# A table of due-time shifts per kind and stretch for a list-scheduled attention and two dense layers

## The chip, the cores and the metric

The kernel runs on one core of one Trainium2 chip. The metric is the device time of one execution in microseconds. Three executions of the kernel before took 1125.41, 1126.01 and 1126.11 us; their median is 1126.01 us.

## What is computed

Attention with normalised queries and keys, its output regrouped to 1792 tokens of width 768, and two dense layers of inner width 2048. All is float32, and the second dense layer takes the first one's output:

```python
attn = softmax(rmsnorm(q, g_q) @ rmsnorm(k, g_k).T / sqrt(64)) @ v   # 4 batches x 12 heads, 448 x 64
x = attn.transpose(0, 2, 1, 3).reshape(1792, 768)
h = x @ moe_w_in                   # 768 x 2048
x = (h * sigmoid(h)) @ moe_w_out   # 2048 x 768
h = x @ moe2_w_in
return (maximum(h, 0) ** 2) @ moe2_w_out
```

## The kernel before

**Numbers in two parts.** TensorE works on fp32r values, and a float32 operand is split into an upper part (a cast, line 578 on ScalarE or 580 on VectorE) and a lower part (operand minus upper part, line 587, on VectorE or GpSimd). A product is three matmuls: upper weight with upper data, lower weight with upper data, upper weight with lower data.

**Stages.** First the attention, 24 pairs of heads. Then the first dense layer in eight segments (two halves of the tokens by four quarters of the inner width), named `seg0` to `seg7` here. A segment has products into the inner width (lines 1082 and 1171), silu (1095, 1239), splits `g_hi`, `g_lo`, and products back (1269), whose sums go to a tile `part`. Then the second dense layer, two halves of the tokens, eight groups of 256 inner columns each: products (1171), relu (1437), square (1443, 1445), splits `h_hi`, `h_lo`, products back (1512, 1636), and `acc` (1528, 1531), which adds them to `gg`. Most products into the inner width come in sevens (`seven`, lines 1159 to 1219): seven half-sized products of sums of blocks stand for eight. `p1_copy` (566) takes the first one out of its bank, and `u_sum` (1186) adds the others from theirs; four tiles `g` hold the sums. The sums of the weights are `w_sum` (1128, 1147), and their parts are `w_hi`, `w_lo`. Sums of the data are `y_sum` (1322, 1376), and their parts are `y_hi`, `y_lo`. In the last group of all, 15 additions of kind `join` (1688) put partial sums together. The layers' raw weights are brought into shape by `magnitude` (980), `low` (985) and `merge` (992).

**Who sets the order.** Everything is first put down as steps of a `Plan` (lines 136 to 414). A step has a kind, a place `when` (a segment's number, or a nominal time in the second layer), the engines that may run it with a modelled duration on each, and the steps that it needs. `forward` (221) then issues them one by one. Of the steps whose needs are issued it takes the one with the earliest modelled start, and among equal starts the one with the smallest due time. That is line 262:

```python
k = (st, due[n], n)
```

So a due time decides only between steps that wait for a free engine together. Where a step may run on two engines, the other one is taken if it would end it earlier, and that comparison counts the steps ahead of it by due time. The loads `load_raw2` and `load_y` also don't start before their due time less 25 us (`hold`). `backward` (324) gives each step the time that it has left until the end, and `schedule` (372 to 405) goes through `forward` and `backward` eight times. Its due times are shifted by a table `DUE`, per kind and for four coarse stages, and the round with the shortest modelled span is kept. The attention's steps are pinned to nominal times and aren't ordered by due times. `issue` (407) emits the instructions in the order found, one fixed sequence for each engine; SyncE's queue carries nearly all DMAs in the same way.

**Buffers that matter below.** `p1` uses one PSUM bank of its own (bank 7, tag `pv`), the other products of a seven use three (`t`), products back use four (`s`). The split weights `w` have five buffers, the raw weights two.

Of the kernel before, what the change touches and what calls it, by code (L numbers as in the profile page):

```python
# [110 lines left out]
class Step:  # L111
# [18 lines left out]
    "now": {"ident": 5.75, "swap_pools": -0.5},  # L130
    "seg0": {"add": -0.5, "down": 3, "g_hi": 0.5, "g_lo": 0.75, "keep": 10.25, "load_raw": -6, "load_y": 0.5, "low": 1, "magnitude": -2, "merge": -6, "out1": -1, "p1_copy": 4, "part": 0.5, "prod": 4.75, "silu": 0.5, "store_y": -1, "u_sum": 2.75, "up": 2.5, "w_hi": 4.5, "w_lo": 6.25, "w_sum": -2, "y_hi": 0.75, "y_lo": 1, "y_sum": 2},
    "seg1": {"add": -4.25, "down": -4.5, "g_hi": 2.25, "g_lo": 5, "keep2": 45.25, "load_raw2": 6, "load_word": -5.5, "load_y": -0.75, "low2": -1.5, "magnitude2": -3, "merge2": -4.5, "p1_copy": -6.25, "part": -3.75, "prod": -3.25, "silu": -5.75, "store_y": 7, "u_sum": 2.25, "w_hi": 1.75, "w_lo": 1, "w_sum": -3, "y_hi": 10, "y_lo": 0.75, "y_sum": 2.5},
}


class Plan:
# [235 lines left out]
    def schedule(self):  # L372
        self.link()
        steps = self.steps

        at = [s.at for s in steps]
        due = [0.0] * len(steps)
# [17 lines left out]
        due = [d + x for d, x in zip(due, moved)]  # L395
        best = None
        got = [None]
        for _ in range(ROUNDS):
            got = self.forward(due, got[0])
            if best is None or got[0] < best[0]:  # L400
                best = got
            late = self.backward(got[1], got[2])
            due = [x - y for x, y in zip(moved, late)]
            self.log = getattr(self, "log", []) + [round(got[0], 1)]
        return best

    def issue(self):
        self.span, start, at, order = self.schedule()
# [1344 lines left out]
```

## Time and profile before

| | |
|---|---|
| median of three executions | 1126.01 us |
| the profiled execution's own time | 1125.93 us |
| its span, first to last instruction | 1124.2 us |
| TensorE busy | 1099.9 us, 98% |
| VectorE busy | 912.9 us, 81% |
| ScalarE busy | 617.2 us, 55% |
| GpSimd busy | 291.7 us, 26% |
| mean granted TensorE clock | 0.995 |

The profile comes from one execution. 1.73 us of that execution's time lie outside its span. A matmul's end is modelled and runs into the next one, so what counts for TensorE is the time in which nothing runs on it, and the distance from one start to the next. Attention takes up to 222.6 us of the span, the dense layers go from there to 1120.6 us, and what is left is the store of the last results. `seg1` lies at about 282 to 340 us, `seg2` at 340 to 396, `seg3` at 396 to 450, `seg4` from 450; the second layer begins at about 676 us, and its second half at about 900 us.

### The profile page before, as it was taken

What the parts mean: (1) busy time and instruction counts of PE and PEld (TensorE: products, weight loads), DVE (VectorE), ACT (ScalarE), POOL (GpSimd) and SP (SyncE); (2) the same over time, 40 slices, a digit from 0 to 9 for tenths busy, and PEclk for the clock granted to TensorE, in tenths of its full rate; (3) what the DMA queues carried; (4) which work ended last, traced back from release to release, by engine and by line L of the source; (5) the groups of instructions that cost most, each with busy time, mean ns of one, the idle gap of its engine ahead of it and who ended that gap; (6) DMA issues with size and microseconds to landing.
All of it is one profiled execution on the core that took longest, in us unless ns stands there. A gap on an engine that the chain in (4) does not pass through costs nothing.

```text
span 1124.2 us, 20358 instructions
## 1 busy us (share of the span) xinstructions
PE 1099.9 (98%) x7463; PEld 994.6 (88%) x7463; DVE 912.9 (81%) x1619; ACT 617.2 (55%) x1310; POOL 291.7 (26%) x369
## 2 busy tenths in 40 slices
PE   8999999999899999999999999999999999999998
PEld 6777777799798989999999998999999899999997
DVE  7999999767868689867777896688888967888886
ACT  7999999964534355455545534534333444333321
POOL 5789997300101113100000110010220201122220
PEclk9999999999999999999999999999999999999999
DMA  7344543397455658578777488778758784555544
GB/s 187 102 125 142 148 128 104 85 330 231 137 179 158 199 184 273 196 242 268 240 271 250 159 296 328 259 264 322 288 203 307 243 313 176 186 187 185 174 173 129
DMA packets 122435, 235.29 MB, mean 209 GB/s; under 512 B 12216, under 2 KB 86112, under 8 KB 122336
## 3 DMA queue, kind: packets, MB, share of 16 engines
q1 hardware_dynamic: 122096, 233.80, 62.4%
q8 instruction: 59, 0.97, 0.4%
q14 instruction: 40, 0.33, 0.1%
q10 hardware_dynamic: 240, 0.20, 0.1%
HBM read 157.58 MB, written 76.37 MB: 208 GB/s over the span
## 4 chain that ended last, share of the span: by engine, by line
PE 56%; DVE 6%; ACT 1%; issue 1%; DMA 0%; DVEq 0%; ACTq 0%
PE bank L1171 26%; PE bank L1269 13%; PE bank L1512 11%; PE bank L1636 7%; DVE w L587 1%; DVE g L1186 1%; DVE gg L1531 1%; DVE gg L1688 0%; ACT g L1437 0%; ACT g L1443 0%; DVE gl L587 0%; DVE W L1128 0%; DMA y<-g 0%; DVE W L1147 0%; DVE w L580 0%
## 5 line engine op out<-in xcount | busy, mean ns | idle before, releaser
L1269 PE MATMUL bank<-gg,w 128*128 128x448 f32 (+1 forms) x1168 | 238.3, 363 | 0.0
L1269 PEld LDWEIGHTS bank<-gg,w 128*128 128x128 f32 x1168 | 216.9, 188 | 16.8
L1186 DVE TENSOR_TENSOR g<-bank,g 128x448 f32<-128x448 f32 x180 | 109.1, 619 | 68.2 <-PE bank L1171 60.3
L1512 PE MATMUL bank<-w,gh 128*128 128x384 f32 (+1 forms) x564 | 143.7, 336 | 1.9 <-DVE gh L580 0.9
L1171 PE MATMUL bank<-yb,w 128*128 128x448 f32 (+1 forms) x548 | 121.1, 369 | 5.3 <-DVE w L587 2.4
L1171 PE MATMUL bank<-xb,w 128*128 128x448 f32 x528 | 116.2, 365 | 3.2 <-ACT g L566 3.2
L1531 DVE TENSOR_TENSOR gg<-bank,gg 128x384 f32<-128x384 f32 (+1 forms) x197 | 102.9, 548 | 20.0 <-PE bank L1512 19.7
L587 DVE TENSOR_TENSOR w<-W,w 128x768 fp32r<-128x768 f32 (+1 forms) x124 | 112.6, 915 | 5.3 <-ACT w L578 4.2
L1171 PEld LDWEIGHTS bank<-yb,w 128*128 128x128 f32 x548 | 102.8, 191 | 15.7 <-DVE w L587 4.0
L1171 PEld LDWEIGHTS bank<-xb,w 128*128 128x128 f32 x528 | 98.1, 188 | 11.7 <-ACT g L566 3.9
L1512 PEld LDWEIGHTS bank<-w,gh 128*128 128x128 f32 x564 | 102.4, 189 | 3.9 <-DVE gg L1531 1.6
L578 ACT CAST w<-W 128x768 fp32r<-128x768 f32 (+1 forms) x82 | 61.5, 750 | 77.9 <-PE bank L1269 21.1
L775 DVE TENSOR_REDUCE mx<-bank 128x1 f32<-128x448 f32 x168 | 96.5, 606 | 0.5 <-PE bank L753 0.5
L1512 PE MATMUL bank<-w,gl 128*128 128x384 f32 (+1 forms) x282 | 94.6, 335 | 1.9 <-DVE gl L587 1.9
L1437 ACT ACTIVATE g<-g 128x448 f32<-128x448 f32 x48 | 27.7, 578 | 123.7 <-DVE g L1186 123.3
L783 ACT ACTIVATE E<-bank,mx 128x448 f32<-128x448 f32 x144 | 93.4, 706 | 0.8 <-DVE mx L775 0.3
L1171 PE MATMUL bank<-xc,w 128*128 128x448 f32 x270 | 60.0, 366 | 0.0
L985 ACT ACTIVATE raw<-raw 128x768 int32<-128x768 uint16 (+1 forms) x72 | 59.2, 824 | 0.0
L587 POOL TENSOR_TENSOR gg<-g,gg 128x448 fp32r<-128x448 f32 x11 | 14.8, 1347 | 169.5 <-ACT gg L578 97.3
L753 PE MATMUL bank<-T 64*128 64x448 f32 x432 | 56.2, 390 | 2.1 <-ACT T L696 1.9
L587 POOL TENSOR_TENSOR gl<-g,gh 128x448 fp32r<-128x448 f32 (+1 forms) x18 | 18.9, 1052 | 150.9 <-ACT gh L578 82.3
L1512 PEld LDWEIGHTS bank<-w,gl 128*128 128x128 f32 x282 | 53.2, 188 | 2.6 <-DVE gl L587 2.6
(180 smaller groups left out, 2242.7 us busy)
## 6 DMA issues: line engine op xcount, KB each, us to landing
raw<-in_moe_w_in_dram SPq DMA_DIRECT2D x32, 768.0 KB
raw<-in_moe_w_out_dram SPq DMA_DIRECT2D x24, 512.0 KB
raw<-in_moe_w_out_dram SPq DMA_DIRECT2D x16, 768.0 KB
su<-w SPq DMA_DIRECT2D x16, 768.0 KB
w<-su SPq DMA_DIRECT2D x16, 768.0 KB
xf<-y SPq DMA_DIRECT2D x48, 224.0 KB
xf<-x SPq DMA_DIRECT2D x39, 224.0 KB
ki<-W SPq DMA_DIRECT2D x16, 384.0 KB
```

Source lines behind the costliest of these rows:

```text
L578: nc.scalar.copy(o(), a())
L587: kind, when, any_t(n, rate), lambda e: engine(e).tensor_tensor(o(), a(), h(), ALU.subtract),
L753: nc.tensor.matmul(pts[j].ap[:, :S], T.ap[r, 0, a, c * CQ:(c + 1) * CQ], T.ap[r, 1, b_], start=(k_ == 0), stop=(k_ == 2),)
L775: lambda e, pt=pt, mx=mx: nc.vector.tensor_reduce(mx.ap, pt.ap[:, :S], AX.X, ALU.max, negate=True),
L783: lambda e, j=j, n=n, pt=pt, mx=mx, E=E: nc.scalar.activation(E.ap[:, j], pt.ap[:, :S], AF.Exp, bias=mx.ap, accum_out=sums.ap[:, n:n + 1]),
L985: lambda e: nc.scalar.activation(lo(), raw.ap[:, :2 * m].bitcast(U16).rearrange("p (m t) -> p m t", t=4)[:, :, 1], AF.Copy, bias=2.0 ** -1 ...
L1171: nc.tensor.matmul(pt.ap[:, c1:c2], w_()[:, c0 + c, :], view(b, a, c)()[:, c1:c2], start=(start and c == 0 and k == 0), stop=(c == HC - 1 ...
L1186: lambda e: nc.vector.tensor_tensor(o.ap, pt.ap[:, :S], a.ap, ALU.add),
L1269: nc.tensor.matmul(pt.ap[:, c1:c2], w_()[:, f, :], gg.ap[:, k, a, f, c1:c2], start=(f == 0 and n == 0), stop=(f == HQ - 1 and n == 2), ski ...
L1512: nc.tensor.matmul(pt.ap[:, :en], g.ap[:, fi, c0:c0 + P], w_()[:, 0, e0:e0 + en], start=(n == 0), stop=(n == 5),)
L1531: "acc", at, dve_t(n), lambda e: nc.vector.tensor_tensor(o(), pt.ap[:, :n], o(), ALU.add),
L1636: nc.tensor.matmul(pt.ap[:, :NH], a[i][0](m), b[j][0](), start=(start and k == 0), stop=(k == 2), skip_group_check=True,)
```

## The change

A table `SHIFT` is added, with 363 entries in 27 stretches: the eight segments, and the second layer cut by nominal time into stretches of an eighth of one half, `end-2` to `end17`. After the eight rounds, `schedule` takes the due times with which the shortest round was made, adds each dense step's entry, runs `forward` once more, and returns that order, whatever its modelled span. A negative entry makes a step more urgent. The entries are between -406.5 and 328.25 us; 98 of them are at most 5 us in size and 140 are over 20. Attention's pinned steps have none. No step, operand, buffer or instruction is added or taken away. The core of the diff, with the stretches that are spoken of below:

```diff
+SHIFT = {
...
+    "seg1": {"add": -11.75, "down": -6, "g_hi": 148, "g_lo": -10.5, "keep": -27.75, "load_raw": -10.5, "low": -7.5, "magnitude": -17.25, "p1_copy": -4.25, "prod": 78.25, "u_sum": 123, "w_hi": 285.25, "w_lo": 29.75, "w_sum": -30.75},
+    "seg2": {"add": 1.5, "down": -99.75, "g_hi": 30, "g_lo": 8, "keep": 22.25, "load_raw": -18.75, "low": -73.75, "magnitude": -0.25, "merge": -0.25, "p1_copy": -42, "prod": 14.5, "silu": 17, "u_sum": 27.75, "w_hi": -10, "w_lo": -55, "w_sum": -52.75},
+    "seg3": {"down": -205.5, "g_hi": -6.5, "g_lo": 90.25, "keep": 33.25, "load_raw": 1.75, "low": -2.25, "magnitude": -1.25, "merge": -26.5, "out1": -8.5, "p1_copy": -9.5, "prod": 86, "silu": -1.75, "store_y": 4.5, "u_sum": -384.5, "w_hi": -37.75, "w_lo": 31.75, "w_sum": 1.75},
+    "seg4": {"down": 9.25, "g_hi": -0.75, "g_lo": -3.25, "keep2": -23.75, "load_raw2": -7.25, "load_word": -15, "load_y": 8, "low2": 2.25, "magnitude2": 1, "merge2": 10.5, "p1_copy": 28.25, "part": 13.5, "prod": 2, "silu": -2, "w_hi": -2.75, "w_lo": 10.75, "w_sum": -13.5, "y_hi": 15.5, "y_lo": -406.5, "y_sum": 155},
+    "seg5": {"add": -41, "down": 69.5, "g_hi": 72.25, "g_lo": 2.5, "keep2": -16, "load_raw2": -136.75, "load_word": -5.5, "low2": 77.25, "magnitude2": -29.5, "merge2": 163.25, "p1_copy": 3.5, "prod": 29, "silu": 10, "u_sum": -10.5, "w_hi": 17.75, "w_lo": 10.25, "w_sum": -101.75},
...
+    "end0": {"acc": 0.5, "down2": 3, "h_lo": -10.25, "load_word2": 4.25, "load_y": 4.5, "p1_copy": 4.25, "prod": 57, "relu": 13, "square": 6.75, "u_sum": 0.75, "w_hi2": -3.25, "w_lo2": 3.5, "w_sum": 14.75, "y_hi": 19.75, "y_lo": 21.5, "y_sum": -3.75},
...
+    "end7": {"acc": 53.25, "down2": 5, "h_lo": -12.25, "keep_parts2": -9.5, "load_word2": -11.75, "p1_copy": 0.75, "relu": -7, "square": 75, "u_sum": 29.25, "w_hi2": -5.75, "w_lo2": -18.75, "w_sum": 5.25},
+    "end8": {"down2": -9, "h_hi": 3, "h_lo": -3.25, "load_word2": 47, "load_y": 5, "relu": -7.5, "square": 1, "store": -13.5, "w_hi2": -36.5, "y_hi": 45.75, "y_lo": 53.75, "y_sum": 0.25},
...
+    "end16": {"acc": -38.5, "down2": -62.25, "h_hi": -1, "h_lo": -4.25, "join": 1.5, "load_parts2": 0.5, "p1_copy": 3, "prod": -30.5, "relu": -1.75, "u_sum": 20},
...
 }
...
         for _ in range(ROUNDS):
-            got = self.forward(due, got[0])
+            end = got[0]
+            got = self.forward(due, end)
             if best is None or got[0] < best[0]:
-                best = got
+                best, args = got, (due, end)
             late = self.backward(got[1], got[2])
             due = [x - y for x, y in zip(moved, late)]
             self.log = getattr(self, "log", []) + [round(got[0], 1)]
-        return best
+        def part(s):
+            when = s.when[0]
+            if s.nom is not None or when not in ("seg", "end"):
+                return None
+            return when + str(int(s.when[1] if when == "seg" else s.when[1] * 8 / self.turn))
+
+        due, end = args
+        return self.forward([d + SHIFT.get(part(s), {}).get(s.kind, 0.0) for s, d in zip(steps, due)], end)
```

## Rows read from the trace of the kernel before

**Rows 1.** The page's head: each engine's busy time, its share of the span, instructions.

```profile
PE 1099.9 (98%) x7463; PEld 994.6 (88%) x7463; DVE 912.9 (81%) x1619; ACT 617.2 (55%) x1310; POOL 291.7 (26%) x369
```

**Rows 2.** Busy time by stretch; each starts A:B length, then PE, PEld and the rest.

```profile
222.60:1120.60 898.00, 883.54 (x4557) 825.71 (x4557) 710.25 (x1225) 402.68 (x685) 126.31 (x99) 1.00 0.68 230
508.00:676.00 168.00, 168.00 (x847) 156.02 (x846) 135.61 (x225) 84.81 (x133) 14.50 (x10) 1.00 0.75 246
957.00:1091.00 134.00, 134.00 (x709) 125.62 (x709) 110.83 (x215) 45.71 (x85) 28.36 (x28) 1.00 0.53 183
```

**Rows 3.** Waits of PE in the dense layers (total, times, longest us), largest first.

```profile
PE bank L1171 <- ACT g L566: 3.2, 2, 2.5
PE bank L1171 <- DVE w L587: 2.8, 3, 1.9
PE bank L1171 <- ACT g L1437: 2.1, 1, 2.1
PE bank L1512 <- DVE gl L587: 1.9, 1, 1.9
```

**Rows 4.** Busy time around two falls of the clock; PEclk is third from last.

```profile
302.80:306.20 3.40, 3.40 (x11) 3.04 (x10) 2.28 (x4) 2.60 (x5) 0.00 (x0) 0.50 0.23 45
306.20:309.60 3.40, 3.40 (x19) 3.11 (x19) 2.62 (x5) 0.00 (x0) 1.15 (x1) 1.00 0.60 197
691.90:695.30 3.40, 3.40 (x12) 3.13 (x11) 3.40 (x8) 2.31 (x4) 0.00 (x0) 0.50 0.21 87
```

**Rows 5.** Timeline at the longest wait, in seg1: start, length, engine, instruction, [idle before].

```profile
301.33 2.51 PE L1171 MATMUL bank<-xb,w 128*128 128x448 f32 x9 [2.51 <-ACT g L566]
...
300.01 0.83 ACT L578 CAST w<-W 128x768 fp32r<-128x768 f32 x1
300.75 0.53 ACT L566 COPY g<-bank 128x448 f32<-128x448 f32 x1
```

**Rows 6.** Timeline at the wait in seg2, ScalarE.

```profile
357.31 0.82 ACT L578 CAST w<-W 128x768 fp32r<-128x768 f32 x1
358.11 0.53 ACT L566 COPY g<-bank 128x448 f32<-128x448 f32 x1
```

**Rows 7.** Timeline at the wait in seg3, VectorE.

```profile
413.34 0.62 DVE L587 TENSOR_TENSOR gg<-g,gg 128x448 fp32r<-128x448 f32 x1
413.88 0.55 DVE L1147 TENSOR_TENSOR W<-W 128x384 f32<-128x384 f32 x1
414.35 0.62 DVE L1186 TENSOR_TENSOR g<-bank,g 128x448 f32<-128x448 f32 x1
```

**Rows 8.** Timeline at the wait where seg4 begins: PE's wait, and VectorE ahead of it.

```profile
450.62 0.48 PE L1171 MATMUL bank<-gh,w 128*128 128x224 f32 x2 [0.37 <-DVE w L587]
...
449.08 0.62 DVE L1376 TENSOR_TENSOR xf<-xf 128x448 f32<-128x448 f32 x1
449.61 0.95 DVE L587 TENSOR_TENSOR w<-W,w 128x768 fp32r<-128x768 f32 x1
```

**Rows 9.** Timeline at the wait before the second layer's second half, VectorE.

```profile
887.21 1.14 DVE L1186 TENSOR_TENSOR g<-bank,g 128x448 f32<-128x448 f32 x2
888.28 0.54 DVE L1531 TENSOR_TENSOR gg<-bank,gg 128x384 f32<-128x384 f32 x1
888.74 0.60 DVE L1186 TENSOR_TENSOR g<-bank,g 128x448 f32<-128x448 f32 x1
889.27 0.60 DVE L587 TENSOR_TENSOR gl<-g,gh 128x448 fp32r<-128x448 f32 x1
```

**Rows 10.** Timeline at 753 us: VectorE beside GpSimd, and PE's wait behind them.

```profile
752.62 1.40 POOL L587 TENSOR_TENSOR v<-W,v 128x384 fp32r<-128x384 f32 x1
...
753.06 1.77 DVE L587 TENSOR_TENSOR w<-W,w 128x768 fp32r<-128x768 f32 x1
...
755.35 0.62 PE L1512 MATMUL bank<-w,gh 128*128 128x384 f32 x2 [0.48 <-DVE gg L1531]
```

**Rows 11.** Waits in SyncE's queue in the dense layers (total, times, longest us).

```profile
SPq L973 <- DVE W L992: 123.5, 31, 8.8
```

19 lines of the change are left out of this document (added).

## The prediction

> **What bounds the kernel now.** First the page's head: TensorE is busy for 98% of the span, VectorE for 81%, ScalarE for 55% [rows 1]. That share alone does not say how much is left, because a matmul's modelled end runs into the next one. So the second view is busy time by stretch. In the dense part, 222.6 to 1120.6 us, TensorE runs 4557 matmuls and is busy for 883.54 of 898.00 us [rows 2]. The 14.46 us that are missing are all that an order of the same matmuls can win from waits. They are not spread evenly: from 508 to 676 us and from 957 to 1091 us, 302 us together, nothing is missing at all [rows 2]. There a new order can only keep the time or lose some.
>
> The third view is the waits of PE. Ten groups hold the dense part's waits, and the four in rows 3 carry most of them. Four single waits are long: 2.5, 2.1, 1.9 and 1.9 us, 8.4 us of the 14.46 [rows 3]. In each TensorE stands for one late step on ScalarE or VectorE, not for a DMA. The fourth view is the granted clock. It is at full speed but for two stretches of some 3.4 us, at 302.8 and 691.9 us, where it is 0.50, the lower level of 1.2 GHz. In these 11 and 12 matmuls start, against 19 in the same time behind the first of them [rows 4]. Eight matmuls at 3.40 / 19 = 0.18 us each make about 1.4 us lost in each, 2.8 in both. The first fall begins 1.5 us after the end of the longest wait, at 301.33 us [rows 5], and the second stands behind the wait of 2.1 us at the second layer's start; behind the two of 1.9 us there is none. So the dense part has 14.46 + 2.8 = 17.3 us to win, 1.5% of the span, and attention has nothing in this change, since its steps are pinned.
>
> **The change, part by part.** It adds and removes no instruction, so the 4557 matmuls cost what they cost. The front end of the sum is therefore fixed, and only waits and clock can move. What moves is who goes first when several steps wait for one engine. I can't see the new order, but at each wait I can read which step was late, what stood just ahead of it on its engine, and whether the two entries of the table turn that pair round. The time of what stood ahead, from start to start, is then what the late step gains at most.
>
> At 301.33 us, in `seg1`, PE waits 2.51 us for a copy of a bank, `p1_copy` [rows 5]. Just ahead of it ScalarE runs an upper part of weights, `w_hi`, from 300.01 to 300.75, so 0.74 us. The table has -4.25 for the one and +285.25 for the other: the pair turns. Gain 0.74, and the wait falls to 1.8. That is the length after which the clock stayed up elsewhere, so I count the first fall of the clock as gone, 1.4 more. In `seg2` it is the same pair: 357.31 to 358.11 us is 0.80 [rows 6], the entries are -42 and -10, and PE's wait there is what is left of the group of 3.2 us beside the 2.5: 0.7 [rows 3]. Gain 0.7. In `seg3` PE waits 1.9 us for a lower part of weights, `w_lo` [rows 3]. Ahead of it VectorE has a `g_lo` (0.54 us from start to start), a `w_sum` and a `u_sum` [rows 7]. Only the `g_lo` falls behind (+90.25 against +31.75), while `u_sum` with -384.5 stays ahead for certain. Gain 0.54. Where `seg4` begins, `w_lo` (+10.75) stands behind a `y_sum` (+155) of 0.53 us, and PE's wait is 0.37 [rows 8]. Gain 0.37. Before the second layer's second half PE waits 1.9 us for an `h_lo` [rows 3]. Its group starts at 7 times 27.6 us of nominal time, which is `end7`, while its relu, square and splits lie in `end8`. VectorE runs three `u_sum` (887.21 to 888.28 and 888.74 to 889.27, 1.60 us) and an `acc` ahead of it [rows 9]. The entries are +29.25 for `u_sum` and -3.25 for `h_lo`: it passes all three. Gain 1.60, if its upper part is ready by then.
>
> Two waits are not helped. At the second layer's start PE waits 2.1 us for a relu [rows 3], and `end0` makes relu later by 13 us while squares get 6.75 and splits 0 or less: nothing gained there, and the second fall of the clock stays. In the last group `u_sum` gets +20 against +1.5 for `join`, which holds the final chain's sums behind the additions; I price it at nothing, because the chain has the last matmuls in front of it, and at up to 1 us if that cover is gone.
>
> The queues behind the moved steps: each engine runs its own fixed sequence, so a step that is put ahead and isn't ready yet holds all behind it. SyncE's loads move too: in `seg5` the raw loads may be issued 136.75 us sooner. They still wait for one of two raw buffers, as they do now, 31 times and 8.8 us at the longest [rows 11], and the y loads and stores stand behind them. I cost that at nothing, because the waits of PE have no DMA in them now; the bound is one wait of 8.8 us less whatever lead those loads have.
>
> One row bears on GpSimd. At 753.06 us VectorE's `w_lo` takes 1.77 us while GpSimd works beside it, against 0.95 for the same shape alone [rows 8, 10], and PE then waits 0.48 us for the `acc` behind it [rows 10]. The Trainium skill, page "SBUF — State Buffer", section "Who interferes with whom", says that a VectorE instruction with two SBUF inputs and a GpSimd one that reads SBUF share one read port, and that whichever starts first keeps it for its whole length. By that rule a table that moves splits and sums between the two engines can slow VectorE without adding an instruction; it makes the third rival below.
>
> The sum, against the profiled execution's own 1125.93 us, which stands 0.08 us under the median: 0.74 + 1.4 + 0.7 + 0.54 + 0.37 + 1.60 = 5.35 us. 1125.93 - 5.35 = 1120.6 us.
>
> **The rivals.** *Nearly all waits go.* The table has an entry for almost every kind, and the order is rebuilt from the front, so waits that I gave nothing for can go as well. Three quarters of the 17.3 us are 13.0: 1112.9 us. For it: most of the waits are shorter than two VectorE instructions. Against it: the second layer's start, which the table doesn't help.
>
> *Nothing that can be measured.* Due times decide only among steps with one modelled start. If the late steps weren't yet waiting in the plan when the ones ahead were chosen, the pairs above don't turn, and waits go in one place and come in another: about 1125.5 us. For it: PE's waits are where the chip departs from the plan, since a plan would not choose to wait 2.5 us in one place.
>
> *GpSimd takes more steps.* If ten more collisions like that at 753 us stand uncovered, each costs PE 0.48 us: 4.8 us, which eats the gain: about 1125.4 us. For it: GpSimd is busy 126 of the 898 us, so there is room [rows 2]. Against: its waits of PE number one now.
>
> *Slower: heads of queues in the full stretches.* The mechanism is a step that the table has put ahead on VectorE or ScalarE, whose input comes late on the chip and which holds steps behind it that TensorE needs. The place is the 302 us in which no time is missing now [rows 2]; the entries there are large (`seg5` has `g_hi` at +72, `low2` at +77, `merge2` at +163). The price is that of the four long waits, 2.1 us each, and 1.4 for a fall of the clock behind each second one. The Trainium skill, page "TensorE: Matmul & The Clock Gate", section "Architectural detail: the array is 16× 32×32, not 1× 128×128", says that ScalarE and VectorE take their instructions strictly in order, which speaks for this rival; no row here shows an instruction overtaken. It decides from four such waits on: 8.4 + 2.8 = 11.2 less the 5.35 is +5.9 us, 1131.8 us. With two, 4.2 + 1.4 = 5.6 just cancels the gain. Against it: VectorE has 32 of 168 and 23 of 134 us free there [rows 2], so a held step mostly finds slack.
>
> That the change doesn't act is hardly possible: `forward` runs once more with the shifted due times and its order is returned even if the modelled span is longer.
>
> **How the numbers follow.** The forecast of 1120.6 us has a chance of 0.48, nearly all waits going 0.11, nothing measurable 0.13, GpSimd 0.06, slower 0.22. A measurement of this kernel can tell about 0.2%, 2.3 us, from no change. So faster is 0.48 + 0.11 = 0.59, the same 0.13 + 0.06 = 0.19, slower 0.22. The forecast's own range runs from 1116 (twice the gain, less a little) to 1123.5. The range for 8 in 10 goes from 1112, where three quarters of what can be won are won, to 1130, just over where three of the four waits of the slower rival come (6.3 + 2.1 - 5.35 = 3.1 us more); it leaves out the deepest gains and the heavier half of the slower case.
>
> **What would show it.** Right: TensorE's idle time in the dense part falls from 14.46 to about 10.5 us; one fall of the clock is left, at the second layer's start; the waits for `p1_copy` in `seg1` and `seg2`, and that before the second half, are shorter or gone; the two full stretches stay full. Wrong: new waits of PE in these stretches, a third fall of the clock, more and longer VectorE instructions beside GpSimd, or a wait of PE behind a DMA. If idle time falls where the pairs didn't turn, the forecast may be right in size and its steps wrong.

## The result, and the profile after

Four executions of the changed kernel took 1114.12 to 1116.25 us, median 1114.99; four of the kernel before, beside them, 1125.89 in the median. The ratio is 0.9905, 95% interval 0.9887 to 0.9922: 10.9 us faster. The forecast was 1120.6, so the direction held, the time lies in the range, and the gain was twice what was forecast. The profiled execution of after took 1114.12 us, its span is 1112.3, and its mean granted clock 0.998; the other three had 0.997, 0.995 and 0.995. One execution of a later kernel, raw_moved, took 1534 us at a mean clock of 0.654 and is left out of its median.

First the page's head of after, against [rows 1]: the same 7463 matmuls, and each engine's busy time within 2%.

```profile
PE 1094.0 (98%) x7463; PEld 991.0 (89%) x7463; DVE 910.7 (82%) x1629; ACT 615.9 (55%) x1308; POOL 287.0 (26%) x361
```

Then the stretches of after, as [rows 2] are those of before (A:B, length, PE, PEld, DVE, ACT, POOL, granted clock, DMA share, GB/s).

```profile
222.60:1108.70 886.10, 878.72 (x4572) 823.91 (x4569) 706.15 (x1231) 402.37 (x684) 121.50 (x91) 1.00 0.68 232
508.00:676.00 168.00, 166.99 (x840) 154.43 (x839) 133.77 (x220) 80.34 (x127) 25.74 (x18) 1.00 0.75 248
957.00:1091.00 134.00, 133.31 (x714) 126.64 (x713) 113.92 (x219) 45.55 (x87) 37.09 (x34) 1.00 0.52 179
```

In the dense part TensorE now lacks 7.38 us, where it lacked 14.46, and no fall of the clock lies in it in this execution, where there were two [rows 4]. The second and third line are the stretches in which nothing was missing before: 1.01 and 0.69 us are missing now.

The five largest groups of waits of PE in the dense layers of after (total, times, longest). Line numbers of after are those of before plus 38: 1209 stands for 1171, 1550 for 1512.

```profile
PE bank L1209 <- DMA w<-sw: 2.0, 1, 2.0
PE bank L1307 <- DVE gg L625: 1.4, 2, 1.0
PE bank L1674 <- DVE part L625: 1.2, 3, 0.7
PE bank L1550 <- DVE gh L618: 0.9, 1, 0.9
PE bank L1209 <- ACT g L1277: 0.5, 1, 0.5
```

None of the four groups of [rows 3] is left; the longest wait is a new one, for a DMA. What a wait costs is best read from the starts of the matmuls on both sides of it, less the usual distance of two starts (203 ns for 448 columns, 174 for 384). By that measure, place by place:

| place (us where the wait begins in before) | before | after |
|---|---|---|
| start of the dense layers, 222.7 | 0.8 | 0, but it starts 1.1 later |
| seg1, 286 | 1.5 | 0 |
| seg1, 298 | 2.7, and a fall of the clock | 0.6 |
| seg2, 358 | 0.8 | 0 |
| seg3, 414 | 2.1 | 1.8 in three waits, at 424 to 428 |
| seg4, 450 | 0.5 | 0 |
| seg7, 648 in after (full before) | 0 | 1.2 |
| second layer's start, 689 | 2.3, and a fall of the clock | 0 |
| 729, 754, 832 | 1.6 in three | 0 |
| ahead of the second half, 888 | 2.0 for an `h_lo` | 2.1 for a load, at 876 |
| second half | 2.8 in four | 3.9 in seven |

The waits sum to 17.1 us before and 9.6 after, the two falls to 2.8 and 0. That is 10.3 us of the 13.0 by which the dense part is shorter; most of the rest lies in starts that are 0.02 to 0.25 us late: 57 in before, which sum to 5.3 us, and 40 in after, which sum to 3.5. 1.1 us are lost again because attention ends later.

Why it ends later shows in its last stretch. Before and after, TensorE waits there for a reciprocal, `sum`, on VectorE; the first line is of before, the others are of after, the last of them a stretch as above:

```profile
218.50 0.22 PE L823 MATMUL bank<-ident,sum 64*7 64x64 f32 x2 [0.40 <-DVE sum L830]
...
215.02 1.39 DVE L618 CAST w<-W 128x768 fp32r<-128x768 f32 x1
216.45 0.96 DVE L625 TENSOR_TENSOR w<-W,w 128x768 fp32r<-128x768 f32 x1
...
218.77 0.22 PE L861 MATMUL bank<-ident,sum 64*7 64x64 f32 x2 [1.74 <-DVE sum L868]
...
219.20:222.60 3.40, 3.40 (x20) 2.01 (x18) 1.48 (x5) 1.95 (x3) 0.00 (x0) 0.51 0.53 192
```

The splits of a dense weight now stand on VectorE ahead of attention's last steps, and the clock is 0.51 behind the wait. All nine kernels in which entries of `seg0` for the engines' steps are in force wait 1.73 to 1.85 us there, the eleven others 0.40 or 0.41. `rest`, which has this wait and no fall of the clock up to there, starts its first dense product at 222.23 us; turned, which has neither, at 221.23. So these entries cost 1.0 us ahead of the dense layers, and a fall of the clock where one comes.

### The profile page after: what moved, and what is told of

The parts are those of the page before. It is cut to its first block, busy times and chain, and to the rows that moved or that the text cites. A ratio compares the mean times of both kernels' runs of the same rounds, so it can differ in the third digit from the quotient of the medians.

```text
span 1112.3 us, 20308 instructions
## 1 busy us (share of the span) xinstructions
PE 1094.0 (98%) x7463; PEld 991.0 (89%) x7463; DVE 910.7 (82%) x1629; ACT 615.9 (55%) x1308; POOL 287.0 (26%) x361
## 4 chain that ended last, share of the span: by engine, by line
PE 87%; DVE 7%; issue 2%; ACT 1%; DMA 1%; SPq 0%; POOL 0%; DVEq 0%; ACTq 0%
PE bank L1209 29%; PE bank L1307 20%; PE bank L1550 13%; PE bank L901 7%; PE bank L1674 6%; PE bank L791 4%; PE bank L834 3%; PE bank L1120 3%; PE bank L725 2%; DVE g L1224 1%; PE bank L798 1%; DVE w L625 1%; DVE gg L625 1%; DVE W L1030 1%; DMA w<-sz 0%
## 5 line engine op out<-in xcount | busy, mean ns | idle before, releaser
L1209 PE MATMUL bank<-yb,w 128*128 128x448 f32 (+1 forms) x548 | 118.1, 363 | 0.5 <-ACT g L1277 0.5
L616 ACT CAST w<-W 128x768 fp32r<-128x768 f32 (+1 forms) x86 | 64.4, 752 | 96.2 <-PE bank L1550 28.1
L625 DVE TENSOR_TENSOR w<-W,w 128x768 fp32r<-128x768 f32 (+1 forms) x121 | 105.8, 880 | 6.0 <-ACT w L616 4.9
L625 POOL TENSOR_TENSOR gl<-g,gh 128x448 fp32r<-128x448 f32 (+1 forms) x16 | 14.6, 914 | 188.3 <-ACT gh L616 110.1
L625 POOL TENSOR_TENSOR gg<-g,gg 128x448 fp32r<-128x448 f32 x6 | 7.9, 1315 | 183.7 <-ACT gg L616 176.3
L1209 PEld LDWEIGHTS bank<-xc,w 128*128 128x128 f32 x270 | 50.7, 188 | 4.3
```

The source lines that it names most:

```text
L616: nc.scalar.copy(o(), a())
L625: kind, when, any_t(n, rate), lambda e: engine(e).tensor_tensor(o(), a(), h(), ALU.subtract),
L1209: nc.tensor.matmul(pt.ap[:, c1:c2], w_()[:, c0 + c, :], view(b, a, c)()[:, c1:c2], start=(start and c == 0 and k == 0), stop=(c == HC - 1 ...
```

## The experiments

Each kernel is compared with runs of the kernel before on the same chip; both medians stand in the table, and a gain or loss in us is their difference. "Idle" is TensorE's idle time from 222.60 us to 3.60 us ahead of the span's end, in the one profiled execution: 14.46 in before, 7.38 in after. In turned, only_dma and group the dense layers begin 1.1 to 1.5 us sooner, so their first wait, 0.5 us, lies ahead of that stretch.

| kernel | time, us | before, us | ratio to before, 95% | idle |
|---|---|---|---|---|
| seg_only | 1121.88 | 1125.66 | 0.9966 [0.9954, 0.9978] | 10.25 |
| end_only | 1125.39 | 1125.66 | 1.0002 [0.9993, 1.0012] | 16.12 |
| pairs | 1138.28 | 1125.66 | 1.0121 [1.0106, 1.0136] | 22.95 |
| rest | 1125.05 | 1125.66 | 1.0003 [0.9993, 1.0012] | 13.63 |
| w_hi_later | 1126.87 | 1125.93 | 1.0008 [0.9996, 1.0019] | 15.04 |
| seg_and_y | 1120.41 | 1125.93 | 0.9958 [0.9943, 0.9973] | 9.52 |
| no_y | 1122.06 | 1125.93 | 0.9969 [0.9959, 0.9980] | 11.65 |
| shuffled | 1174.38 | 1125.93 | 1.0432 [1.0411, 1.0453] | 46.79 |
| raw_behind | 1122.13 | 1125.30 | 0.9973 [0.9963, 0.9983] | 12.72 |
| to_end8 | 1117.12 | 1125.30 | 0.9923 [0.9910, 0.9937] | 8.34 |
| no_dma | 1134.71 | 1125.30 | 1.0078 [1.0064, 1.0092] | 20.12 |
| only_dma | 1123.72 | 1125.30 | 0.9984 [0.9975, 0.9993] | 12.01 |
| turned | 1122.14 | 1126.12 | 0.9965 [0.9952, 0.9978] | 12.98 |
| relu_up | 1125.30 | 1126.12 | 0.9994 [0.9983, 1.0005] | 14.05 |
| raw_moved | 1126.10 | 1126.12 | 0.9998 [0.9986, 1.0011] | 14.39 |
| turned_relu | 1122.87 | 1126.12 | 0.9975 [0.9965, 0.9986] | 13.69 |
| group | 1121.35 | 1125.84 | 0.9961 [0.9947, 0.9974] | 11.71 |
| after_g_lo | 1114.79 | 1125.84 | 0.9901 [0.9888, 0.9915] | 7.46 |

### Halves of the table, and the forecast's ten entries

**seg_only** keeps the entries of the first layer, **end_only** those of the second.

```diff
 # seg_only; end_only is the other way round
-    "end-2": {"load_y": -17.25, "y_hi": 328.25, ...},
+    "end-2": {},
...
```

> Only the eight segments' entries; the second layer has none. In the traces of before and after, starts of matmuls come 10.9 us too late in all between 222 and 676 us before, and 4.8 us after. If the stretches act each by itself, this run keeps the 6.1 us of the first layer and nothing else: about 1119.8 us, with the wait of 2.1 us and the fall of the clock at the second layer's start still there. If the entries of both layers only work together (the second layer's steps are fitted to an order that this kernel also has at their start), the second layer may wait more than before: 1122 us or over.

> Only the second layer's entries. From 676 us on, matmuls start 14.4 us too late in all before and 8.1 us after. If the stretches act each by itself: 6.3 us faster than before, about 1119.6 us, with the waits of 2.5, 0.7, 1.9 and 0.4 us in seg1 to seg4 as before and no fall of the clock at the second layer's start. If the entries need each other: less than half of that, 1123 us or over.

Neither half is worth what was expected, and together they are worth three times the sum of what they are alone: 3.8 and 0 us. Up to seg7 seg_only has nearly the waits of after (one of 0.45 us, at 594, is its own); then the wait at seg7's end, 1.0 us in after and none in before, is 3.7. Its largest group of waits of PE:

```profile
PE bank L1307 <- DVE gg L625: 4.0, 2, 3.7
```

end_only has the waits of before up to 450 us, each the same within 0.02 us from start to start. The wait at the second layer's start is gone from it, but 2.0 us come at 744, 1.1 at 782, 1.7 at 804 and 2.2 for a load at 888.

**pairs** has only the ten entries whose pairs the forecast counted, **rest** all but these.

```diff
 # pairs: all that is left of the table
+    "seg1": {"p1_copy": -4.25, "w_hi": 285.25},
+    "seg2": {"p1_copy": -42, "w_hi": -10},
+    "seg3": {"g_lo": 90.25, "w_lo": 31.75},
+    "seg4": {"w_lo": 10.75, "y_sum": 155},
+    "end7": {"u_sum": 29.25},
+    "end8": {"h_lo": -3.25},
```

> Only the ten entries on which the forecast's sum rests: p1_copy and w_hi of seg1 and seg2, g_lo and w_lo of seg3, y_sum and w_lo of seg4, u_sum of end7, h_lo of end8. If a wait shortens because the step just ahead of the late one falls behind it: 5.35 us faster than before, about 1120.5 us, and those five waits shorter by 0.74, 0.7, 0.54, 0.37 and 1.6 us. If the two steps of a pair weren't waiting together when the planner chose, the pairs don't turn: the five waits stand at their places as before, or others come with a changed order, and the time is 1125 us or over.

> The whole table without those ten entries. If the forecast's pairs carry 5.35 of the 10.9 us: about 1120.3 us, with the five waits back. If what works is the order that all entries make together: at most a few of the five waits are back, the wait at the second layer's start stays away, and the time is 1115 to 1118 us.

The ten entries that the forecast credited with 3.95 us and a fall of the clock made the kernel 12.6 us slower, and the other 353 alone gain nothing. In the timeline of pairs at the longest wait, in seg1 (start, length, engine, instruction, idle before), against [rows 5]:

```profile
301.38 1.15 DVE L625 TENSOR_TENSOR gg<-g,gg 128x448 fp32r<-128x448 f32 x2
301.43 0.55 ACT L616 CAST gg<-g 128x448 fp32r<-128x448 f32 x1
301.88 0.83 ACT L616 CAST w<-W 128x768 fp32r<-128x768 f32 x1
302.45 0.61 DVE L606 COPY g<-bank 128x448 f32<-128x448 f32 x1
303.12 1.86 PE L1209 MATMUL bank<-xb,w 128*128 128x448 f32 x4 [3.63 <-DVE g L606]
```

`w_hi` did go later. But a `g_hi` took its place on ScalarE, and `p1_copy` went to VectorE instead, behind two `g_lo`: the wait for it grew from 2.51 to 3.63 us. An entry of the table doesn't simply turn a pair. It changes what the planner takes next among all the steps that wait, and on which engine.

### The pairs turned by hand

**turned** therefore turns the same five pairs in the finished order of before. No table; every other instruction keeps its place on its engine.

```diff
+TURN = [
+    (1947, "ahead", 1944),   # seg1: p1_copy ahead of w_hi
+    (2121, "ahead", 2118),   # seg2: p1_copy ahead of w_hi
+    (2265, "behind", 2293),  # seg3: g_lo behind w_lo
+    (2468, "behind", 2495),  # seg4: y_sum behind w_lo
+    (3901, "behind", 3900),  # end7: h_lo ahead of the three u_sum
+    (3903, "behind", 3901),  # end7: u_sum behind h_lo
+]
```

> The kernel before's order with nothing but the forecast's five pairs turned by hand: in seg1 and seg2 p1_copy ahead of w_hi on ScalarE, in seg3 g_lo behind w_lo on VectorE, where seg4 begins y_sum behind w_lo, before the second layer's second half h_lo ahead of the three u_sum. No table, and no other step moves. If the forecast's terms were sized rightly and only the way from an entry of the table to a turned pair was wrong: PE's waits there fall from 2.5, 0.7, 1.9, 0.4 and 1.9 us by 0.7, 0.7, 0.5, 0.4 and 1.6, the fall of the clock behind the first goes in most executions, and the time is the forecast's 1120.6 us (1119.5 to 1122). If a turned pair only hands the wait to the step that is now behind, as in the kernel that had these entries alone: 1125 us or more, with new waits of PE just behind the five places.

It is 4.0 us faster, between the two that were expected. The terms can be read one by one (start to start). seg1: 2.68 to 1.86, but 0.47 come right behind it. seg2: 0.83 stays. seg3: 2.07 to 1.39. seg4: 0.53 to 0.41. Ahead of the second half: 2.04 to 0.95, but 0.29 and 1.57 come behind. The timeline of turned in seg1, in seg2, and twice ahead of the second half:

```profile
298.53 0.51 ACT L566 COPY g<-bank 128x448 f32<-128x448 f32 x1
298.94 0.84 ACT L578 CAST w<-W 128x768 fp32r<-128x768 f32 x1
299.09 2.09 PE L1171 MATMUL bank<-xb,w 128*128 128x448 f32 x9 [1.70 <-ACT g L566]
...
301.69 1.48 PE L1171 MATMUL bank<-yb,w 128*128 128x448 f32 x6 [0.31 <-DVE w L587]
...
354.84 0.53 ACT L566 COPY g<-bank 128x448 f32<-128x448 f32 x1 [0.69 <-PE bank L1171]
...
881.43 2.11 DVE L587 TENSOR_TENSOR gl<-g,gh 128x448 fp32r<-128x448 f32 x2
881.91 1.16 POOL L1322 TENSOR_TENSOR xf<-xf 128x448 f32<-128x448 f32 x1 [2.62 <-DMA xf<-y]
...
888.27 2.22 POOL L587 TENSOR_TENSOR xb<-V,xb 128x768 fp32r<-128x768 f32 x1
888.72 2.25 DVE L587 TENSOR_TENSOR xc<-xf,xc 128x448 fp32r<-128x448 f32 x1
891.59 0.59 PE L1512 MATMUL bank<-w,gh 128*128 128x384 f32 x2 [1.41 <-DVE gg L1531]
```

In seg1 the copy gains what the forecast gave it, and the lower part of the weights, whose upper part is now second, becomes late. In seg2 the copy stands first and waits 0.69 us for TensorE itself: its bank wasn't done. `w_hi` ahead of it [rows 6] had cost nothing. Ahead of the second half the `h_lo` passes the three `u_sum` and an `acc` between them, 2.06 us from start to start, but now runs beside GpSimd: the two `gl` at 881.43 take 2.11 us, the second 1.57 where it took 0.60 in before, and of the 2.06 only 1.09 are left. Further on VectorE's `xc` takes 2.25 us beside GpSimd, against 0.61 us for the same shape at 885.53. Before has this too, at 893.01 us with 2.26. What is new is that the three `u_sum` and the `acc` stand behind the `h_lo`: from its end to the `acc` that TensorE needs next it is 7.4 us, where it was 5.3. The page "SBUF — State Buffer" of the Trainium skill, section "Who interferes with whom", gives VectorE and GpSimd one shared pair of ports that one of them holds at a time; these rows agree.

In turned's profiled execution the clock never falls below 1.00, and the three executions with that clock took 1120.45 to 1121.62 us. The waits as a whole shrank little: the lateness of all dense matmuls sums to 22.3 us in before, its two falls left out, and to 22.2 in turned. So much of the 4.0 us is clock; but at a mean clock of 0.997 turned took 1123.2 and 1123.4 us and before 1124.1 to 1125.4, which leaves some 1.4 us that are not.

### The start of the second layer

The forecast called the wait of 2.1 us there "not helped". It is gone in after, and in seg_only, which has no entry there at all. Four theories were tried in turn. **w_hi_later** asked if two entries of `end1` hold the cause, **raw_behind** if the raw load that stands ahead of the last store of `y` in SyncE's queue does.

```diff
 # w_hi_later: all that is left of the table
+    "end1": {"w_hi2": 79, "w_lo2": 89.5},
```

> Two entries alone: w_hi2 and w_lo2 of end1 (+79 and +89.5). At the second layer's start the kernel before has, on VectorE, a w_hi2 of the next group just ahead of four u_sum; it stands 1.92 us for PE to give a buffer free, and the u_sum behind it, though their banks are full, stand with it. In this kernel that cast goes to ScalarE, behind the relu, and nearly nothing else moves. If a step that waits at the head of an in-order queue made the wait of 2.1 us and the fall of the clock behind it: both are gone, 2.1 + 1.4 = 3.5 us less, about 1122.2 us. If it was the relu's place among the squares and splits on ScalarE, as the forecast read it: the wait stays, and the time is that of before within 0.5 us.

```diff
 # raw_behind: the order of before, planned anew with one more condition
+            if s.kind == "load_raw2" and first - 2.0 < got[1][s.n] < got[1][last.n]:
+                self.pre[s.n].append((last.n, False))
+                self.post[last.n].append((s.n, False))
```

> The kernel before with one pair of DMAs in SyncE's queue turned round: the raw load that it issues at 677.50 us, 768 KB, goes behind the last store of the first layer's output, 678.56 us. From 672 to 692 us the DMA engines are full (share 1.00 to 1.04), and the tile g that this store reads is one of the four that the second layer's first sums need. If the wait of 2.1 us at the second layer's start hangs on that store: it lands some 1.9 us sooner, the wait of PE there is at most 0.5 us, and the fall of the clock behind it is gone; about 2 to 3.5 us less, 1122.5 to 1124 us, as later waits change with the order. If it hangs on the relu's place on ScalarE or on a cast at a queue's head: the wait stays at 2.1 us.

In w_hi_later the cast left VectorE, as its entry wanted, and went to the head of ScalarE's queue, where it waited 3.13 us for TensorE to be done with its buffer, the relu behind it. PE's wait stayed at 2.15. raw_behind was 3.2 us faster and the wait was gone. That looked like the cause, but a plan made anew also had ScalarE's order changed. Three further runs took this apart, with edits by hand in the finished order of before: **relu_up** moves one activation, **raw_moved** one load, **group** takes over raw_behind's order and engines for the `u_sum`, `relu`, `square`, `h_hi` and `h_lo` of this one group, and leaves the load where it was. **turned_relu** is turned and relu_up together.

```diff
 # relu_up
+TURN = [(3310, "behind", 3305)]   # the relu that reads a whole bank: second, not fourth relu
 # raw_moved
+TURN = [(3013, "behind", 3192)]   # the raw load behind the last store_y
 # group: 22 steps in another order, five of them on another engine
+MOVED = {3306: "dve", 3307: "act", 3318: "dve", 3324: "act", 3325: "act"}
```

> The kernel before's order with one step moved: at the second layer's start the relu that reads a whole bank goes second among ScalarE's activations there instead of fifth. The raw load stays ahead of the last store of y. If PE's wait of 2.1 us there comes from ScalarE's order: the wait falls to at most 0.5 us, and with it mostly the fall of the clock: 2 to 3.5 us less than before, 1122.4 to 1124 us. If it comes from the store of y that stands behind the raw load and holds a tile: the relu now stands at ScalarE's head until the store has landed, the activations behind it come later, and PE's wait stays at 1.5 us or more: 1125 to 1127 us.

> The kernel before's order with one DMA moved: the raw load that stands ahead of the last store of y in SyncE's queue goes behind it. ScalarE, VectorE, GpSimd and TensorE keep their orders. If ScalarE's order makes the wait at the second layer's start: nothing changes, the wait stays at 2.1 us within 0.3, and the time within 0.1% of before. If the store behind the load makes it: the wait goes as in the kernel in which the plan was made anew with this load behind the store, about 1122 us.

> Both hand edits, the five turned pairs and the relu moved up. If edits of a fixed order add up where entries of the table did not: the gains of the two kernels together, within 0.8 us. If they disturb one another as the parts of the table did, the sum is missed by more than 1.5 us.

> The kernel before's order, in which the second layer's first group alone (its u_sum, relu, square, h_hi and h_lo) goes in the order and on the engines that the plan gives with the raw load behind the last store: the relu of the whole bank second, its h_hi on ScalarE at once, the first square on VectorE, the last one on ScalarE. The raw load and all else stay as they were. If it is the sharing of the whole group between ScalarE and VectorE that makes PE's 2.1 us there: the wait goes, and nothing like the 1.6 and 0.5 us appears behind it as it did when only the relu was moved; 2 to 3.5 us less than before, 1122.5 to 1124 us. If those 3 us came from elsewhere in the new plan: the wait is handed on once more, and the time stays within 0.1% of before.

The timeline of before, ScalarE and the wait:

```profile
687.08 0.58 ACT L1437 ACTIVATE g<-g 128x448 f32<-128x448 f32 x1 [4.36 <-DVE g L1186]
687.69 0.58 ACT L1443 ACTIVATE g<-g 128x448 f32<-128x448 f32 x1
688.31 0.58 ACT L1437 ACTIVATE g<-g 128x448 f32<-128x448 f32 x1
688.92 0.58 ACT L1443 ACTIVATE g<-g 128x448 f32<-128x448 f32 x1
...
690.00 0.57 ACT L1437 ACTIVATE g<-g 128x448 f32<-128x448 f32 x1
690.48 0.52 ACT L1437 ACTIVATE g<-bank 128x448 f32<-128x448 f32 x1
...
691.05 3.06 PE L1171 MATMUL bank<-yb,w 128*128 128x448 f32 x10 [2.15 <-ACT g L1437]
```

TensorE's next product needs the bank that the relu at 690.48 empties, and six instructions stand ahead of that relu since 687.08. raw_moved changes nothing: the wait is 2.15 us again, so the load alone isn't it. relu_up has this relu at 687.79 and no wait here. But at 692 us it has two waits of PE that before doesn't have, one in each of these groups:

```profile
PE bank L1512 <- DVE gh L580: 2.4, 2, 1.5
PE bank L1512 <- DVE gl L587: 2.3, 2, 1.9
```

Start to start they are 1.64 and 0.54 us, 2.18 in all, for the 2.31 that went. The next products want `h_hi` and `h_lo` of the same group, and these are no sooner. The timeline of group:

```profile
685.96 0.58 ACT L1437 ACTIVATE g<-g 128x448 f32<-128x448 f32 x1 [4.92 <-DVE g L1186]
686.44 0.53 ACT L1437 ACTIVATE g<-bank 128x448 f32<-128x448 f32 x1
686.57 0.62 DVE L1445 TENSOR_TENSOR g<-g 128x448 f32<-128x448 f32 x1
...
687.48 0.55 ACT L578 CAST gh<-g 128x448 fp32r<-128x448 f32 x1
...
687.62 2.01 PE L1171 MATMUL bank<-yb,w 128*128 128x448 f32 x10
...
689.47 0.51 PE L1512 MATMUL bank<-w,gh 128*128 128x384 f32 x2
```

The first square runs on VectorE beside the relu of the bank, and ScalarE splits the result at once. Neither the wait nor its heirs are there, and the kernel is 4.5 us faster than before from 22 steps in one place. So in before the 2.1 us belonged to the sharing of a whole group between two engines. The changed kernel has the same beginning: relu, relu of the bank, and a square on VectorE at 680.73 us. seg_only loses the wait by another road: its first squares stay on ScalarE, but TensorE runs nine further matmuls of line 1209 ahead of the products back. turned_relu gains 3.3 us, no more than turned: its two waits at that place, 1.65 and 0.55 us, are those of relu_up.

### What the table's parts do together

**seg_and_y** adds the four entries of `end-2` (the next layer's data, prepared in seg7) to the first layer's, **no_y** takes these four out of the whole table. **to_end8** leaves out the second half of the second layer, 108 entries (its expectation says 116). **no_dma** leaves out the 62 entries of loads, keeps and stores, **only_dma** keeps these alone. **shuffled** has all the table's numbers, dealt anew at random within each stretch.

```diff
 # no_y
-    "end-2": {"load_y": -17.25, "y_hi": 328.25, "y_lo": -2, "y_sum": 24.75},
+    "end-2": {},
 # to_end8: the same for "end9" to "end17"
 # no_dma: without the kinds load_*, keep* and store*; only_dma: these alone
```

> The segments' entries and those of end-2 (the loads, sums and splits of the second layer's first input). The run with the segments alone took 1121.9 us and had a wait of 3.7 us at the end of seg7 for a lower part on VectorE, and a fall of the clock. If these come from the y steps of the second layer, which stand ahead of seg7's g_lo without end-2's entries: that wait falls to about 1 us as in the kernel after, the fall is gone, and the time is 1121.9 - 2.7 - 1.4 = about 1117.8 us or less. If the entries of a stretch act by themselves: 1121.9 us, as with the segments alone.

> The whole table without the four entries of end-2 (load_y, y_hi, y_lo, y_sum). If they are fitted together with seg7: the wait of some 3.7 us at the end of seg7 and a fall of the clock come, 4 us or more over the kernel after, 1119 us or over. If four entries of 363 count by their number: 1115 us.

> The same 363 values, but within each stretch they are dealt out to the kinds at random. If the kernel before had a poor order by chance and nearly any other one would do: 1115 to 1126 us. If the values are fitted to their kinds: slower than before by far more than 1%, as priorities of up to 400 us that mean nothing put late steps ahead of urgent ones: 1140 us or over.

> The table up to end8; end9 to end17, 116 entries, are left out. In the traces the matmuls from 900 us on start 5.6 us too late in all before and some 5.9 us after, with no wait gone and none come that is worth 1 us. If each place has its own price: the time of the kernel after within 0.7 us, 1115 us. If the table only works whole, as the runs without ten or four entries seemed to say: 1120 us or over.

> The table without its 62 entries of loads, stores and keeps; the 301 entries of the engines' and TensorE's steps stay. If the gain comes from the order on VectorE and ScalarE, as the forecast's sum has it: 1115 to 1118 us. If loads and stores have to move along with it, as a load that comes late or in front of a store holds buffers that the new order wants: slower than the kernel after by 5 us or more, and not faster than before.

> Only the 62 entries of loads, stores and keeps. If the gain comes from the order of the DMAs alone: 1115 to 1118 us. If both are needed: about the time of before, within 3 us, with the waits of seg1 to seg4 at their places.

Four entries of 363 are worth 7 us: without them the wait in seg7 is not 1.2 but 4.1 us, and in the profile a fall of the clock comes with it, at 652 us. The largest group of waits of PE of no_y:

```profile
PE bank L1307 <- DVE gg L625: 4.3, 2, 3.9
```

With them seg_and_y has 1.2 there, as after has, but a new wait of 2.4 us at 746, and at 883 it keeps the 2.0 us that before has for an `h_lo`. The entries of the DMAs alone gain 1.6 us, the others alone lose 9.4, both together gain 10.9. to_end8 loses 2.1 us against after, though its waits after 850 us sum to 6.0 us and those of after to 6.2. The loss is in small pieces: a wait of 0.5 us at 806, and many later starts; over all dense matmuls they sum to 15.4 us in its profile, and to 12.9 in after. And the numbers dealt at random cost 48.5 us; the largest group of PE's waits in shuffled:

```profile
PE bank L1307 <- ACT gg L616: 8.7, 1, 8.7
```

So the gain isn't a matter of the table's spread. Its values fit one another, and what a part is worth depends on the order that the others make.

**after_g_lo** asked if the changed kernel can be bettered by hand. In seg7 of after TensorE waits for the last of these:

```profile
646.84 0.61 DVE L625 TENSOR_TENSOR yb<-xf,yb 128x448 fp32r<-128x448 f32 x1
647.38 0.61 DVE L625 TENSOR_TENSOR xb<-xf,xb 128x448 fp32r<-128x448 f32 x1
647.91 0.61 DVE L1360 TENSOR_TENSOR xf<-xf 128x448 f32<-128x448 f32 x1
648.45 0.61 DVE L625 TENSOR_TENSOR gg<-g,gg 128x448 fp32r<-128x448 f32 x1
...
649.11 1.07 PE L1307 MATMUL bank<-gg,w 128*128 128x448 f32 x4 [1.01 <-DVE gg L625]
```

```diff
+TURN = [(3106, "behind", 3100)]   # this g_lo ahead of the three steps above it
```

> The changed kernel with one step moved by hand: in seg7 the g_lo for which PE waits 1.0 us goes ahead of two y_lo and one y_sum on VectorE. If VectorE has room for the three steps behind it: the wait goes and the time falls by about 1.1 us, from 1115.0 to about 1113.9 us, the lower of both kernels. If they are needed as soon: the wait is handed on to the loads of y or to the second layer's start, and the time stays or rises by up to 2 us.

In its profile the wait for the `g_lo` is gone and a wait of 1.2 us stands 1 us later, at 650.35, for the sum that empties a bank (`g`, line 1320) and now comes behind the three steps. 1114.79 us can't be told from 1114.99. No run was faster than the changed kernel by more than the measurement tells.

## Why the prediction was right in its sign and half in its size

**The ceiling held.** The prediction had 17.3 us to win in idle time and clock. In the two profiles 7.08 and 2.8 of these went, against the 3.95 and 1.4 it forecast. The stretches with nothing to win lost 1.7 us: late steps on VectorE, as the rival that was to be slower had it, did hold TensorE there, with waits of 1.2 and 0.9 us and not four of 2.1. The wait of 0.9 us, at 991, is of the GpSimd rival's kind: two splits of `part` on VectorE take 1.96 us beside a GpSimd step, where each took 0.55 alone in before. GpSimd ran fewer steps in the dense part as a whole (91 for 99 [rows 2]), but more in the two full stretches (18 for 10 and 34 for 28). That attention "has nothing in this change, since its steps are pinned" was wrong: dense steps share its engines, and their new order cost 1.0 us at its end.

**The size failed in the waits that were put at nothing.** From start to start, the five places that the sum counts lost 8.1 us before and 4.5 after. That is 3.6 us less, close to the forecast's 3.95, and the fall behind the first, 1.4, went too. The agreement is luck, since the pairs were not the road to it (below). The other 6.9 us of the spans' difference of 11.9 the sum put at nothing: 3.7 at the second layer's start with its fall, 3.9 in the short waits at 222.7, 286, 729, 754 and 832 us, 2.7 in small late starts and the rest, less 2.3 for new waits in seg7 and the second half, and 1.1 at attention's end.

**"The time of what stood ahead, from start to start, is then what the late step gains at most"** failed as well. For pairs turned alone it was passed a little twice (turned: 0.82 for 0.74, 0.68 for 0.54) and far from reached three times (0.12 for 0.37, 1.09 for 1.60, 0 for 0.70). It left out three questions: is the late step's own input ready (in seg2 it wasn't), what runs beside it in its new place (the `h_lo` met GpSimd), and what does TensorE want next (0.47 behind the first, 1.86 behind the last). Net, the five pairs by hand gained 2.7 us and handed on 2.3.

**"The two entries of the table turn that pair round"** failed more badly. The ten entries by themselves cost 12.6 us: the planner's choice is made among all steps that wait, and in seg1 the copy changed its engine. So the sign was right, but not by the steps that led to it. In the changed kernel the waits went by another road: in seg1 TensorE no longer waits for the copy at all, but 0.5 us for a silu.

**The second layer's start, "not helped", "nothing gained there".** Right was that a late relu on ScalarE makes it and no DMA (raw_moved). Wrong was to judge by the sizes of `end0`'s entries: the wait goes with no entry there (seg_only), and a new sharing of the group between the engines is enough to remove it (group). The size of what was missed is 2.3 us and the fall behind it.

**The 1.60 for `h_lo`.** That wait did go, and one of 2.0 us came in its stead, at 876 us of after, for a load of split weights that SyncE issued at 873.94 us:

```profile
873.94 0.32 SPq L1054 DMA_DIRECT2D w<-sw  x1
...
878.25 2.09 PE L1209 MATMUL bank<-raw,w 128*128 128x448 f32 x10 [1.96 <-DMA w<-sw]
```

The loads were costed at nothing "because the waits of PE have no DMA in them now". That cover was TensorE's own order, which the table shifts too: in before 84 matmuls of the products back run at this place, from 887.54 to 904.31 us, and in after ten matmuls with the loaded weights come first, 4.3 us behind the issue of their load. end_only has the same order and a wait of 2.2 us for the same load, though TensorE isn't sooner there.

**The clock** was the term with the best mechanism. Some 1.4 us a fall is confirmed, but one profile of each kernel does not tell how many falls their medians hold (below). With a mean clock of 0.995 after took 1115.67 and 1116.25 us, before 1125.1 to 1126.9: at the same clock some 10 of the 10.9 us remain, so in the medians the clock gives about 1 us, and not the 2.8 of the two profiles.

**"Nearly all waits go" at 1112.9** was the nearest case, and had a chance of 0.11. It was put low because the second layer's start seemed out of the table's reach. In the profiles 9.9 of the 17.3 us went, not three quarters. Faster by any road had 0.59.

**What stays open.** Which of the 353 other entries carry the gain can't be said, since parts don't add.

## What to carry to other kernels

A wait is a place in a queue: here moving the step that TensorE waited for handed the wait to the next steps of the same group (2.31 us became 2.18), and moving the group, with its sharing between two engines, removed it. For each late step look first whether its own input is ready, then what would run beside it, then what TensorE needs next, before the time of what stands ahead is credited. Parts of a fitted set of priorities need not be worth what they are worth in the whole: here ten entries cost 12.6 us, more than all 363 gain, so an estimate by pairs gave neither the road nor the size.

## What the runs showed of the chip that was not expected

The same waits bring a fall of the clock in one execution and none in another. The longest wait of before, 2.68 us in seg1, stands in the orders of before, end_only, w_hi_later, relu_up, raw_moved and group, each time within 0.02 us; five of these six profiles have a fall of the clock at or behind it, raw_moved has none. In turned and turned_relu, where the wait is 1.86, there is none either. Here are w_hi_later behind that wait, and at three more places, and then raw_moved behind it (A:B, length, PE, PEld, DVE, ACT, POOL, granted clock, DMA share, GB/s):

```profile
301.60:305.00 3.40, 2.90 (x8) 2.60 (x9) 3.40 (x6) 2.45 (x6) 0.00 (x0) 0.50 0.00 0
417.70:421.10 3.40, 3.40 (x10) 2.98 (x10) 2.85 (x6) 2.46 (x5) 1.42 (x1) 0.50 0.16 40
694.10:697.50 3.40, 3.40 (x12) 3.18 (x11) 3.40 (x8) 2.42 (x4) 0.00 (x0) 0.51 0.24 101
892.10:895.50 3.40, 3.40 (x12) 3.40 (x12) 2.09 (x5) 1.33 (x3) 2.65 (x2) 0.50 1.00 417
```

```profile
302.80:306.20 3.40, 3.40 (x18) 3.16 (x17) 3.15 (x6) 2.56 (x5) 0.00 (x0) 1.00 0.28 78
```

Four of w_hi_later's waits, of 2.68, 2.07, 2.3 and 2.0 us, had 1.2 GHz at their end or behind them, two of the same four in before, and only one in raw_moved. The kernel before itself, over 32 executions, has a mean clock of 0.997 with 1124.1 to 1125.4 us, 0.995 with 1125.7 to 1126.5, 0.994 with 1127.3 to 1127.4 and 0.991 or 0.992 with 1128.2 to 1129.8. The means of neighbouring levels are 0.9 to 1.4 us apart, near the price of one fall that [rows 4] gave. Not every fall lies in the dense part: before's profile has a third, at 12.7 us, in attention. The forecast read from one execution that the two waits of 1.9 us have no fall behind them; in w_hi_later, with the same waits, both have one. The page "TensorE: Matmul & The Clock Gate" of the Trainium skill, section "Part 1: The HAM clock gate", says of the slow matmuls at a kernel's start that their number differs from run to run; the rows here show the same of falls in a kernel's middle.
